# One tile of x turned by the DMA crossbar instead of TensorE, and a gate column read as rows

## The chip, the core and the metric

The kernel runs on one core of a Trainium2 chip. The metric is device time in microseconds of one execution, the median of several runs. The profile is of one further execution; its times count from the start of that execution's span. Five engines have instruction queues of their own: TensorE (PE: matmuls; PEld: its weight loads), VectorE (DVE), ScalarE (ACT), GpSimd (POOL) and SyncE (SP). DMAs are issued from the queues of SP, ACT or POOL and are carried by 16 DMA engines which all queues share.

## The reference

The input x has 2048 tokens of 640 features, in bf16. A linear attention block with 32 heads of 20 features (A) and a gated mixer with an MLP (B) are both computed from x, and a gate per token mixes them.

```python
g = _sigmoid((x * gate_w).sum(-1, keepdims=True))
...
qkv = (x @ wqkv) ...            # (640, 1920)
phi = lambda t: jnp.where(t > 0, t + 1, jnp.exp(t)) + 1e-6
pq, pk = phi(q), phi(k)
kv = jnp.einsum("bhsd,bhse->bhde", pk, v)
z = jnp.einsum("bhsd->bhd", pk)
o = einsum(pq, kv) / (einsum(pq, z)[..., None] + 1e-6)
a = o.reshape(B, S, D) @ wo
...
h = _gelu(_layernorm(x) @ w1)                    # shifted along the tokens in four groups, then @ w2
x1 = x + hs
b = x1 + _gelu(_layernorm(x1) @ w3) @ w4
return g * a + (1 - g) * b
```

For the change it matters that the products x @ wq, x @ wk and the sum x * gate_w all need x with its features on the partitions (turned), because TensorE contracts over partitions.

## The kernel before, in words

The 2048 tokens are cut into 16 x tiles of 128 tokens (x_tok, one tile of 128 tokens by 640 features each). The features are cut into five slices of 128 (KD = 5). The turned form, xT, holds for each slice 128 features on the partitions by all tokens. A Q product of a tile is five pairs of matmuls, one pair per slice: the slice of xT is the stationary operand, and the slice of wq gives 512 and 128 columns (L893 and L894). A K product is the same with wkg, whose last two columns are a column of ones and the gate weights (columns D and D+1), so the K product also gives each token's sum of x and its sum of x * gate_w; ScalarE copies the two to lr for the layer norm and the gate.

The first four x tiles are loaded one by one; tiles 4 to 7, 8 to 11 and 12 to 15 come in three large loads. Tiles 0 to 3 are turned on TensorE: t_x (L758) issues five transposes (L617) into a PSUM bank, and VectorE copies the result to xT (L671). Tiles 4 to 15 are turned by DMA: SP issues a crossbar transpose for each (L703; recorded at L285). The other DMAs are recorded at L289, or at L288 for the gate column.

The order of the first stage is written out by hand. TensorE runs a warm-up of matmuls on constants (L861), transposes tile 0, and then q_four (L900) runs through a list of (tile, slice) entries: an entry (t, None) turns tile t, an entry (t, k) issues the pair of Q matmuls of tile t and slice k, and the stream (L877) calls phi after the fifth slice of a tile. phi is an Exp on ScalarE followed by two operations on VectorE. Then come k_first (L909; recorded at L914) for the K product of tile 0 and k_tile for the others, followed by the Q and K products of tiles 4 to 15. In stream an entry (None, None) issues a small warm-up, which q_four's list does not use.

SP issues in this order: x tiles 0, 1, 2, wq slice 1, x tile 3, wq slices 2 to 4, the five slices of the K weights, the gate column (640 single values, one to each partition and slice), then x tiles 4 to 7 and their transposes, and so on. ScalarE's queue issues wq slice 0 first, and has no other work until the first Exp.

Waits are not written by hand: a small scheduler class records which bytes each operation reads and writes, and puts semaphore waits where they are needed (PSUM banks are locked to the engine that touched them last). Each engine runs its own list in order. A planner (_Items.run) places all later items by modelled times: an item is taken when its inputs are estimated to be ready, so modelled durations of early operations can influence the order of later ones. PSUM banks are also picked by those modelled times.

Of the kernel before, what the change touches and what calls it, by code (L numbers as in the profile page):

```python
# [5 lines left out]
BF16 = mybir.dt.bfloat16  # L6
F32 = mybir.dt.float32
ACTF = mybir.ActivationFunctionType
# [3 lines left out]
D = 640  # L12
# [5 lines left out]
KD = D // 128  # L18
# [398 lines left out]
def _build(nc, A_x, A_wqkv, A_wo, B_w1, B_w2, B_w3, B_w4, gate_w, out, dbg=None, stop=None):  # L417
    sch = _Sched(nc)
# [37 lines left out]
    pa = Arena(SB_LO, SB_HI - SHARED)  # L456
# [3 lines left out]
    ps = nc.alloc_psum_tensor("ps", [128, 8, 512], F32)  # L460
# [6 lines left out]
    ident = pa.alloc("ident", [128, 128], BF16)  # L467
# [11 lines left out]
    x_tok = pa.alloc("x_tok", [128, NT, D], BF16)  # L479
# [10 lines left out]
    junk = pa.alloc("junk", [128, 1, D], BF16)  # L490
    qprod = pa.alloc("qprod", [128, D], F32)
    zacc = qprod
    zsum = pa.alloc("zsum", [128, D], BF16)
    zT = ones_c[:, :].rearrange("p (k f) -> p k f", f=128)
    zf = pa.alloc("zf", [128, KD], BF16)
    xT = ra.alloc("xT", [128, KD, S], BF16)
    GT = ra.alias("GT", [128, KD, D], BF16, ra.last_addr, KD * S * 2)
    wkg = ra.alloc("wkg", [128, KD, NK], BF16)
# [21 lines left out]
    def bank():  # L520
        best = None
        for k_ in range(nbanks[0]):
            b = (bank_rr[0] + k_) % nbanks[0]
            if b in bank_pend or b in bank_hold:
                continue
            lk = sch.locks.get(b)
            tfree = 0.0 if lk is None else sch.ev_time.get((lk[1].sem, lk[1].val), 1e18)
            if best is None or tfree < best[0]:
                best = (tfree, b)
        bank_rr[0] = best[1] + 1  # L530
        bank_pend.add(best[1])
        return best[1]
# [30 lines left out]
    def nfree(ap):  # L563
        n = 1
        for d_ in ap.shape[1:]:
            n *= d_
        return n

    def in_psum(ap):
        return ap.tensor.name == ps.name  # L570

    def act(fn, reads, writes, cost=None):
        if cost is None:
            n = nfree(writes[0])
            cost = max(150.0, 100.0 + 0.833 * n + (70.0 if (reads and in_psum(reads[0])) else 0.0))
            cost += 45.0 * max(0, len(reads) - 1)
        return sch.op("act", fn, reads, writes, cost=cost)
# [13 lines left out]
    def pe(fn, reads, writes, cost=500.0, after=None):  # L591
        for w_ in writes:
            sp_, rl = sch.rects(w_)
            if sp_ == "ps":
                for (_p0, _p1, lo, hi) in rl:
                    for b in range(lo // PS_BANK, (hi - 1) // PS_BANK + 1):
                        bank_pend.discard(b)
        return sch.op("pe", fn, reads, writes, cost=cost, after=after)

    def mm_group(out_ap, pairs, reads_extra=()):  # L600
        n = len(pairs)

        def fn(e, out_ap=out_ap, pairs=pairs, n=n):
            ins = None
            for i, (l, r) in enumerate(pairs):
                ins = e.matmul(out_ap, l, r, start=(i == 0), stop=(i == n - 1))  # L606
            return ins
        reads = [a for p in pairs for a in p] + list(reads_extra)
        return pe(fn, reads, [out_ap], cost=n * (max(nfree(pairs[0][1]), 24) * 0.4167 + 2.5))
# [39 lines left out]
    def activation(out_ap, in_ap, func, scale=1.0, bias=0.0, accum=None):  # L649
        rd = [in_ap] + [a for a in (scale, bias) if not isinstance(a, (int, float))]  # L650
        wr = [out_ap] + ([accum] if accum is not None else [])
        n = nfree(out_ap)
        cost = max(150.0, 100.0 + 0.833 * n + (70.0 if in_psum(in_ap) else 0.0)) + 45.0 * (len(rd) - 1)
        if accum is not None:
            cost += 91.0
        st_ = ACT_SET.get(func)
        if st_ is not None and st_ != sch.act_func:
            cost += 1290.0
            sch.act_func = st_
        if accum is not None:  # L660
            return act(lambda e: e.activation(out_ap, in_ap, func, bias=bias, scale=scale, accum_out=accum), rd, wr, cost=cost)  # L661
        return act(lambda e: e.activation(out_ap, in_ap, func, bias=bias, scale=scale), rd, wr, cost=cost)  # L662

    def memset(engf, ap, val):
        return engf(lambda e: e.memset(ap, val), [], [ap])

    def copy(engf, out_ap, in_ap):
        cost = None
        if engf is dve and in_ap.dtype == BF16 and out_ap.dtype == BF16:
            cost = 65.0 + nfree(out_ap) / 1.92  # L670
        return engf(lambda e: e.tensor_copy(out_ap, in_ap), [in_ap], [out_ap], cost=cost)  # L671
# [7 lines left out]
    def dma_in(out_ap, in_ap, key, **kw):  # L679
        return sch.dma("sp", out_ap, in_ap, key, **kw)  # L680

    def load_x(t, queue="sp"):
        sch.dma(queue, x_tok[:, t, :], x2[128 * t:128 * (t + 1), :], "x%d" % t)

    def load_wq(k, queue="sp"):
        sch.dma(queue, wq[:, k, :], A_wqkv[128 * k:128 * (k + 1), 0:D], "wq%d" % k)

    memset(pool, wkg[:, :, D:D + 2], 1.0)
    load_wq(0, "act")
    for t in range(3):  # L690
        load_x(t)
    load_wq(1)
    load_x(3)
    for k in range(2, KD):
        load_wq(k)
    for k in range(KD):
        dma_in(wkg[:, k, 0:D], A_wqkv[128 * k:128 * (k + 1), D:2 * D], "wk%d" % k)
    dma_in(wkg[:, :, D + 1:D + 2], gate_w.rearrange("(k p o) -> p k o", p=128, o=1), "gw", noncontig=True)
    for c in range(1, NCH):
        for u in {1: (1,), 2: (2, 3)}.get(c, ()):  # L700
            dma_in(x_tok[:, 4 * u:4 * u + 4, :], x2[512 * u:512 * (u + 1), :].rearrange("(n p) d -> p n d", p=128), "xc%d" % u)
        for t in range(4 * c, 4 * c + 4):
            sch.dma("sp", xT[:, :, 128 * t:128 * (t + 1)], x_tok[:, t, :], "trx%d" % (t % 4), transpose=True)  # L703

    k_done = {}

# [49 lines left out]
    WARM2 = 128  # L756
# [94 lines left out]
    def one(n):  # L851
        return nc.const_aps.tensor(1.0, [128, n], BF16)

    def warmup(cols, cyc):
        b = bank()
        steps = [512] * (cols // 512) + [128] * (cols % 512 // 128)

        def fn(e):
            ins = None
            for n in steps:  # L860
                ins = e.matmul(ps[:, b, 0:n], one(128), one(n), start=True, stop=True)  # L861
            return ins
        pe(fn, [], [ps[:, b, :]], cost=cols * cyc)
# [13 lines left out]
    def stream(order, w, n2, done):  # L877
        bs = {}
        for t, k in order:
            if k is None:  # L880
                if t is None:
                    warmup(WARM2, 0.42)
                else:
                    t_x(t)
                continue
            if k == 0:
                bs[t] = pair()
                bank_hold.update((bs[t], bs[t] + 1))
            b = bs[t]
            l = xT[:, k, 128 * t:128 * (t + 1)]  # L890

            def fn(e, l=l, b=b, k=k):
                e.matmul(ps[:, b, 0:512], l, w[:, k, 0:512], start=(k == 0), stop=(k == KD - 1))  # L893
                return e.matmul(ps[:, b + 1, 0:n2], l, w[:, k, 512:512 + n2], start=(k == 0), stop=(k == KD - 1))  # L894
            pe(fn, [w[:, k, 0:512 + n2], l], [ps[:, b, 0:512], ps[:, b + 1, 0:n2]], cost=272.0)
            if k == KD - 1:
                bank_hold.difference_update((b, b + 1))
                done(t, b)

    def q_four():  # L900
        order = [(0, 0), (1, None), (2, None), (1, 0), (0, 1), (1, 1), (2, 0), (2, 1), (3, None), (0, 2), (1, 2), (0, 3), (0, 4), (1, 3),
                 (1, 4), (2, 2), (2, 3), (2, 4), (3, 0), (3, 1), (3, 2), (3, 3), (3, 4)]
        stream(order, wq, 128, lambda t, b: phi(b, pq_tok[:, t + 1, :]))

    def k_out(t, b):
# [16 lines left out]
    addA(("tx", 0), 0.28, lambda: t_x(0, (0, 1, KD)))  # L922
    addA(("warm", 1), 0.0, lambda: warmup(WARM2, 0.42))
    addA(("q", 3), 5.44, q_four)
    addA(("k", 0), 1.36, k_first)
    for i in range(1, 4):
# [349 lines left out]
    for c in range(NCH):  # L1276
        for j in range(KD):
            deps = [(("t1", u), 0.9) for u in range(4 * c, 4 * c + 4)] if j == 0 else []
# [6 lines left out]
    for t in range(NT):  # L1285
        c = t // 4
        deps = [(("w1", c, KD - 1), GEL)]
# [8 lines left out]
    for u in range(NT):  # L1296
        deps = [(("s2", u // 4), 3.2 + 0.9 * (u % 4))]
# [8 lines left out]
    for c in range(NCH):  # L1306
        for j in range(KFF):
            deps = []
# [4 lines left out]
            if j == 0:  # L1313
                deps = deps0 + [(("t2", u), 0.9) for u in range(4 * c, 4 * c + 4)]
# [11 lines left out]
    for t in range(NT):  # L1326
        deps = [(("zb",), 1.0), (("qr", max(t // 4, 1)), 2.0)]
# [14 lines left out]
    for t in range(NT):  # L1342
        c = t // 4
        deps = [(("qt", t), 3.0), (("w4load",), 0.0), (("mq",), 1.0), (("mt",), 2.5)]
# [31 lines left out]
    order = IT.run(sch, hook)  # L1376
# [42 lines left out]
```

## Time and profile before

| | us |
|---|---|
| median of 3 runs | 260.21 |
| lowest, highest | 259.76, 260.26 |
| profiled execution | 260.06 |
| its span | 258.3 |

The time of an execution lies 1.8 us above its span. The granted TensorE clock was 1.0. In the profile's lines, a row of the timeline starts with the start time and the duration in us; "x5" is the number of instructions put together; in brackets stands the idle time before the instruction, and what ended it. A row of waits names the engine, its instruction, what it waited for, and then the total in us, how often, and the longest. A row of DMA issues names destination and source, the queue, how many, the KB of each, and the median us from issue to landing. A row of the table by stretches gives the stretch, the busy time of PE, PEld, DVE, ACT and POOL with their instructions, and last the granted clock, the busy share of the 16 DMA engines (which can pass 1 where packets overlap) and GB/s.

### The profile page before, as it was taken

How to read it: one execution, taken by the hardware profiler on the slowest of the kernel's cores; microseconds unless marked ns; L12 is line 12 of the kernel's file. 1: busy time of each engine (PE TensorE's matmuls, PEld its weight loads, DVE VectorE, ACT ScalarE, POOL GpSimd, SP SyncE). 2: the span in 40 equal slices, each digit the busy share in tenths (PEclk: the TensorE clock that was granted, in tenths of full speed). 3: DMA queues.
4: the chain of work that ended last, by engine and by line, in shares of the span. 5: the costliest groups of instructions: out<-in, count | busy, mean ns of one | idle time of the engine just before them, and what ended most of it. 6: DMA issues, size and time to landing. Idle time of an engine off the chain costs nothing.

```text
span 258.3 us, 3824 instructions
## 1 busy us (share of the span) xinstructions
PE 254.8 (99%) x1427; PEld 122.7 (47%) x1427; DVE 158.2 (61%) x293; ACT 110.9 (43%) x229; POOL 96.8 (37%) x154
## 2 busy tenths in 40 slices
PE   7999999999999999999999999999999999999996
PEld 3555555544444554554444444444444444444443
DVE  2597877899954699989995302999022530134076
ACT  1496777751355857684874240005500045200100
POOL 8014996869934119659681210111020120021000
DMA  6857997826527699483668512114200140000224
GB/s 194 263 101 235 139 141 193 231 55 119 102 49 105 124 392 305 82 101 65 127 124 117 102 20 23 25 25 130 42 3 0 20 124 0 0 0 1 43 84 139
DMA packets 58644, 26.78 MB, mean 104 GB/s; under 512 B 49966, under 2 KB 57215, under 8 KB 58626
## 3 DMA queue, kind: packets, MB, share of 16 engines
q1 hardware_dynamic: 57122, 22.92, 42.5%
q0 software_dynamic: 1168, 3.28, 5.4%
q10 hardware_dynamic: 336, 0.35, 0.4%
q8 instruction: 11, 0.18, 0.3%
q14 instruction: 7, 0.06, 0.1%
HBM read 12.09 MB, written 2.67 MB: 57 GB/s over the span
## 4 chain that ended last, share of the span: by engine, by line
PE 97%; DMA 1%; DVE 0%; issue 0%
PE ps L606 61%; PE ps L1233 22%; PE ps L812 7%; PE ps L893 2%; PE ps L792 1%; DMA x_tok<-in_A_x_dram 1%; PE ps L1120 1%; PE ps L1208 1%; PE ps L617 1%; PE ps L914 1%; PE ps L894 0%; PE ps L984 0%; PE ps L793 0%; PE ps L1213 0%; PE ps L1017 0%; DVE xT L671 0%
## 5 line engine op out<-in xcount | busy, mean ns | idle before, releaser
L606 PE MATMUL ps<-xnT,w 128*128 128x512 bf16 x360 | 81.3, 379 | 0.0
L606 PEld LDWEIGHTS ps<-xnT,w 128*128 128x128 bf16 x360 | 34.6, 98 | 39.3
L645 DVE SCALAR_TENSOR_TENSOR x_tok<-ps,stg,abx 128x512 bf16<-128x512 f32 (+2 forms) x17 | 12.2, 718 | 58.5 <-PE ps L1233 58.4
L1233 PE MATMUL ps<-w,h2T 128*128 128x512 bf16 (+2 forms) x221 | 47.2, 366 | 0.0
L628 POOL TENSOR_SCALAR abx<-x_tok,stg 128x512 f32<-128x512 bf16 x16 | 12.0, 753 | 88.2 <-DVE x_tok L645 70.1
L628 POOL TENSOR_SCALAR xn<-x_tok,st 128x640 bf16<-128x640 bf16 x32 | 38.6, 1215 | 8.6 <-DMA xnT<-xn 8.2
L662 ACT ACTIVATE h2T<-ps 128x512 bf16<-128x512 f32 x52 | 29.9, 599 | 22.7 <-PE ps L606 22.6
L1233 PEld LDWEIGHTS ps<-w,h2T 128*128 128x128 bf16 x221 | 21.2, 98 | 24.1
L662 ACT ACTIVATE tlT<-ps 128x512 bf16<-128x512 f32 x8 | 4.8, 597 | 64.1 <-PE ps L606 41.9
L662 ACT ACTIVATE Er<-ps 128x640 bf16<-128x640 f32 (+1 forms) x35 | 22.9, 658 | 17.8 <-PE ps L606 9.7
L661 ACT ACTIVATE junk<-x_tok 128x640 bf16<-128x640 bf16 x32 | 23.6, 737 | 4.7 <-DVE x_tok L643 4.2
L662 ACT ACTIVATE hsT<-ps 128x512 bf16<-128x512 f32 (+1 forms) x32 | 18.9, 593 | 14.2 <-PE ps L606 13.8
L606 PE MATMUL ps<-w,hsT 128*128 128x512 bf16 (+1 forms) x160 | 24.0, 299 | 0.0
L606 PE MATMUL ps<-wkg,xT 128*128 128x512 bf16 (+1 forms) x150 | 22.6, 299 | 0.0
L606 PE MATMUL ps<-M_sb,pqnT 128*128 128x512 bf16 x80 | 19.7, 379 | 0.0
L606 PEld LDWEIGHTS ps<-w,hsT 128*128 128x128 bf16 x160 | 13.4, 98 | 12.5
L645 DVE SCALAR_TENSOR_TENSOR abx<-ps,stg,abx 128x512 f32<-128x512 f32 x16 | 12.0, 750 | 10.7 <-PE ps L606 7.2
L606 PEld LDWEIGHTS ps<-wkg,xT 128*128 128x128 bf16 x150 | 12.6, 97 | 11.7
L643 DVE SCALAR_TENSOR_TENSOR x_tok<-ps,x_tok 128x640 bf16<-128x640 f32 x16 | 13.1, 821 | 7.6 <-PE ps L606 6.9
L812 PE MATMUL ps<-pk_tok,x_tok 128*128 128x512 bf16 x80 | 17.8, 379 | 0.0
L636 DVE TENSOR_TENSOR qprod<-qprod,pk_tok 128x640 f32<-128x640 f32 x13 | 16.3, 1252 | 0.5
L628 DVE TENSOR_SCALAR Er<-Er 128x640 bf16<-128x640 bf16 (+1 forms) x35 | 11.6, 332 | 7.6 <-ACT Er L662 6.8
(85 smaller groups left out, 282.9 us busy)
## 6 DMA issues: line engine op xcount, KB each, us to landing
w<-in_B_w_dram SPq DMA_DIRECT2D x1, 2160.0 KB, 9.5
w<-in_B_w_dram SPq DMA_DIRECT2D x1, 2080.0 KB, 15.0
x_tok<-in_A_x_dram SPq DMA_DIRECT2D x3, 640.0 KB, 5.6
out_dram<-x_tok SPq DMA_DIRECT2D x3, 640.0 KB, 3.5
w<-in_B_w_dram POOLq DMA_DIRECT2D x8, 160.0 KB, 6.2
wkg<-in_A_wqkv_dram SPq DMA_DIRECT2D x5, 160.0 KB, 3.9
wv<-in_A_wqkv_dram POOLq DMA_DIRECT2D x1, 800.0 KB, 5.6
x_tok<-in_A_x_dram SPq DMA_DIRECT2D x4, 160.0 KB, 3.2
```

Source lines behind the costliest of these rows:

```text
L606: ins = e.matmul(out_ap, l, r, start=(i == 0), stop=(i == n - 1))
L617: ins = e.transpose(o, s_, ident[:])
L628: return engf(lambda e: e.tensor_scalar(out_ap, in_ap, s1, s2, op0, op1), rd, [out_ap], cost=cost)
L636: return engf(lambda e: e.tensor_tensor(out_ap, a, b_, op), [a, b_], [out_ap], cost=cost)
L643: return dve(lambda e: e.scalar_tensor_tensor(out_ap, in0, scalar, in1, op0, op1, accum_out=accum), rd, [out_ap, accum], cost=cost + 70.0)
L645: return dve(lambda e: e.scalar_tensor_tensor(out_ap, in0, scalar, in1, op0, op1), rd, [out_ap], cost=cost)
L661: return act(lambda e: e.activation(out_ap, in_ap, func, bias=bias, scale=scale, accum_out=accum), rd, wr, cost=cost)
L662: return act(lambda e: e.activation(out_ap, in_ap, func, bias=bias, scale=scale), rd, wr, cost=cost)
L792: e.matmul(ps[:, b, :], l, x_tok[:, t, 0:512], start=(t == 0), stop=(t == NT - 1))
L812: ins = e.matmul(ps[:, b, :], l, r, start=(t0 + q_ == 0), stop=(t0 + q_ == NT - 1))
L893: e.matmul(ps[:, b, 0:512], l, w[:, k, 0:512], start=(k == 0), stop=(k == KD - 1))
L1233: ins = e.matmul(o, l, r, start=False, stop=(i == KFF - 1), skip_group_check=shared)
```

## The change

x tile 3 is no longer turned on TensorE. ScalarE's queue issues a crossbar transpose of it, after a small Exp on a constant that brings the load of the activation table to an earlier place. All transposes issued by SP now wait for that one. The Q products of tiles 0 to 2 are reordered and tile 3's come last, as before, in five pairs together.

The gate weights are no longer read into wkg as a column of 640 single values. They are read as five rows of 128 (gw5), from ScalarE's queue behind wq slice 0; one matmul with a 5 by 5 identity turns them into PSUM, and VectorE copies the five columns into wkg. In q_four's list this stands at an entry (None, None), which now means gate_turn.

```diff
+    gw5 = pa.alloc("gw5", [KD, 128], BF16)
...
     load_wq(0, "act")
+    sch.dma("act", gw5[:, :], gate_w.rearrange("(k p) -> k p", p=128), "gw")
     for t in range(3):
         load_x(t)
     load_wq(1)
     load_x(3)
     for k in range(2, KD):
         load_wq(k)
+    activation(junk[:, 0, 0:1], nc.const_aps.tensor(1.0, [128, 1], BF16), ACTF.Exp)
+    turned3 = sch.dma("act", xT[:, :, 384:512], x_tok[:, 3, :], "tr3", transpose=True)
     for k in range(KD):
         dma_in(wkg[:, k, 0:D], A_wqkv[128 * k:128 * (k + 1), D:2 * D], "wk%d" % k)
-    dma_in(wkg[:, :, D + 1:D + 2], gate_w.rearrange("(k p o) -> p k o", p=128, o=1), "gw", noncontig=True)
...
-            sch.dma("sp", xT[:, :, 128 * t:128 * (t + 1)], x_tok[:, t, :], "trx%d" % (t % 4), transpose=True)
+            sch.dma("sp", xT[:, :, 128 * t:128 * (t + 1)], x_tok[:, t, :], "trx%d" % (t % 4), transpose=True, deps=[turned3])
...
                 if t is None:
-                    warmup(WARM2, 0.42)
+                    gate_turn()
...
+    def gate_turn():
+        b = bank()
+        mm_group(ps[:, b, 0:KD], [(gw5[:, :], ident[0:KD, 0:KD])])
+        copy(dve, wkg[:, :, D + 1:D + 2], ps[:, b, 0:KD].unsqueeze(2))
+
     def q_four():
-        order = [(0, 0), (1, None), (2, None), (1, 0), (0, 1), (1, 1), (2, 0), (2, 1), (3, None), (0, 2), (1, 2), (0, 3), (0, 4), (1, 3),
-                 (1, 4), (2, 2), (2, 3), (2, 4), (3, 0), (3, 1), (3, 2), (3, 3), (3, 4)]
+        order = [(0, 0), (1, None), (2, None), (None, None), (1, 0), (0, 1), (1, 1), (2, 0), (2, 1), (0, 2), (1, 2), (2, 2), (0, 3), (1, 3),
+                 (0, 4), (1, 4), (2, 3), (2, 4), (3, 0), (3, 1), (3, 2), (3, 3), (3, 4)]
```

## The prediction

> **What bounds the kernel now.** I read the shares of busy time and the chain that ended last on the page first.
>
> ```profile
> span 258.3 us, 3824 instructions
> PE 254.8 (99%) x1427; PEld 122.7 (47%) x1427; DVE 158.2 (61%) x293; ACT 110.9 (43%) x229; POOL 96.8 (37%) x154
> PE 97%; DMA 1%; DVE 0%; issue 0%
> ```
>
> TensorE is busy for 254.8 of 258.3 us and is 97% of the chain. A microsecond taken off TensorE's stream is worth a microsecond, and so is one of waiting put into it. Next, the waits of TensorE over the whole span:
>
> ```profile
> PE ps L861 <- PEq L1404: 0.8, 1, 0.8
> PE ps L893 <- DVE xT L671: 0.3, 1, 0.3
> PE ps L617 <- DMA x_tok<-in_A_x_dram: 0.2, 1, 0.2
> ```
>
> These are all of them: the start (0.8), x tile 0's arrival (0.2), and one wait for the copy of x tile 1's transposes (0.3, just before 6.21 us). After that TensorE never waits, so nothing downstream can absorb a new wait: it moves the end by its whole length. The change acts in the first 12 us, so I read that part of the timeline.
>
> ```profile
> 5.66 0.89 DVE L671 COPY xT<-ps 128x640 bf16<-128x640 bf16 x2 [0.71 <-PE ps L617]
> 6.21 0.39 PE L893 MATMUL ps<-wq,xT 128*128 128x512 bf16 x1 [0.31 <-DVE xT L671]
> 7.53 0.32 PEld L617 LDWEIGHTS ps<-ident,x_tok 128*128 128x128 bf16 x5
> 7.58 0.44 PE L617 MATMUL ps<-ident,x_tok 128*128 128x128 bf16 x5
> 7.80 0.10 PEld L893 LDWEIGHTS ps<-wq,xT 128*128 128x128 bf16 x1
> 10.25 0.10 PEld L893 LDWEIGHTS ps<-wq,xT 128*128 128x128 bf16 x1
> 10.30 0.38 PE L893 MATMUL ps<-wq,xT 128*128 128x512 bf16 x1
> 11.61 0.37 PEld L914 LDWEIGHTS ps<-wkg,xT 128*128 128x128 bf16 x3
> ```
>
> From 6.21 us on the Q products run in steps of 0.27 us (6.21, 6.49, 6.76 ...), each a 512-column and a 128-column matmul. The five transposes of x tile 3 stand at 7.53 between two steps. Tile 3's own products are the last five of the twenty: their first weight load is at 10.25, and the K products begin at 11.61.
>
> **The change, part by part.**
>
> *Transposes of tile 3 leave TensorE.* Weight loads go on at 7.80 instead of 7.53, and the chain in order of time gives the same piece:
>
> ```profile
> 7.74 0.28 PE ps L617 x5
> ```
>
> I take −0.27 us. The copy after them (0.49 us on VectorE at 8.06) was not waited for, so it is worth nothing. With it gone, tile 3's first weight load would come at 10.25 − 0.27 = 9.98 us.
>
> *The new order of the Q products.* The same twenty pairs are issued, so the sum of work is the same. The third slice of wq is wanted at 7.58 us instead of 7.86, the fourth still at 8.40, the fifth at 8.95 instead of 8.67.
>
> ```profile
> 2.65 0.43 SPq L289 DMA_DIRECT2D x_tok<-in_A_x_dram  x1
> 3.12 1.39 SPq L289 DMA_DIRECT2D wq<-in_A_wqkv_dram  x3
> x_tok<-in_A_x_dram SPq DMA_DIRECT2D x1, 160.0 KB, 4.1
> wq<-in_A_wqkv_dram SPq DMA_DIRECT2D x1, 160.0 KB, 4.1
> ```
>
> Issued at 3.12 and 4.1 us to landing, the third slice is there at 7.2; the later two, about 0.48 us apart, at 7.6 and 8.1. All are 0.3 to 0.8 us early, so the order costs nothing. If that cover went, the loss would be the lateness itself.
>
> *The gate column's matmul.* One weight load and one 5-column matmul come behind tile 2's transposes, which end at about 5.90, inside the 0.31 us in which TensorE waits for the copy. A transpose of 128 columns takes 0.055 us (0.28/5) and a weight load 0.10, so up to 0.15 us fits. Cost: 0. It waits for the gate rows, issued from ScalarE behind wq's first slice, at about 1.24 us. Their landing is bounded by the 2.9 us of x tile 0 and the 4.6 us of the old gate column: 4.1 to 5.9 us. Queued behind that wait is all of TensorE. At the upper end it still costs under 0.1 us. The 5-element copy on VectorE stands behind tile 2's copy (ends 6.55) and ahead of work that starts at 9.88; the nearest copy, 128x128, took 0.22 us. It is hidden, and the K products read its column only after 11 us.
>
> ```profile
> 0.80 0.41 ACTq L289 DMA_DIRECT2D wq<-in_A_wqkv_dram  x1
> 1.24 1.28 ACT L662 ACT_TABLE_LOAD   x1 [1.24 <-PEq L1404]
> 9.15 2.06 ACT L662 ACTIVATE Er<-ps 128x640 bf16<-128x640 f32 x3 [6.62 <-PE ps L894]
> x_tok<-in_A_x_dram SPq DMA_DIRECT2D x1, 160.0 KB, 2.9
> wkg<-in_gate_w_dram SPq DMA_DIRECT2D x1, 1.2 KB, 4.6
> 9.88 0.33 DVE L628 TENSOR_SCALAR Er<-Er 128x640 bf16<-128x640 bf16 x1 [1.33 <-ACT Er L662]
> ```
>
> *ScalarE's queue.* It gets the gate rows' issue (0.41), its table load 0.4 us later, one small Exp, a wait for x tile 3 and the issue of the crossbar transpose (1.3 us on SP). x tile 3 lands at 2.65 + 4.1 = 6.75, so ScalarE is free at about 8.1. Queued behind the wait is the first real Exp, at 9.15 before and about 9.4 now. Hidden, with over a microsecond to spare.
>
> *SP's queue and the 16 DMA engines.* SP loses the gate column's issue, so x tiles 4 to 7 are issued 0.48 us sooner. What the column held back shows in the DMA's rate:
>
> ```profile
> 6.93 0.43 SPq L288 DMA_DIRECT2D wkg<-in_gate_w_dram  x1
> 7.41 0.53 SPq L289 DMA_DIRECT2D x_tok<-in_A_x_dram  x1
> 6.00:9.00 3.00, 2.79 (x24) 1.73 (x25) 1.04 (x3) 0.00 (x0) 1.08 (x1) 1.00 1.06 361
> 9.00:11.00 2.00, 2.00 (x17) 1.12 (x15) 1.08 (x3) 1.79 (x3) 0.00 (x0) 1.00 0.79 182
> 13.22 5.48 SPq L285 DMA_TRANSPOSE xT<-x_tok  x4
> 17.66 1.24 PE L606 MATMUL ps<-wq,xT 128*128 128x512 bf16 x5
> ```
>
> At 182 instead of 361 GB/s (the last column) over 2 us, some 1.0 us of transfer went missing. The new transpose takes about 0.9 us of the same engines (below), so tiles 4 to 7 land about when they did. Their first transpose, issued at 13.22 and landed 2.6 us later, is wanted at 17.66: 1.8 us of slack. The K weights' last slice, issued at about 6.45 with 3.9 us to landing, comes at 10.4, up to 11.3 with the transpose ahead of it, and is wanted after 12 us. SP's later transposes also wait for tile 3's; that ends well before 13 us. All this costs 0.
>
> *When tile 3 arrives.* This term decides, and no row of before has a crossbar transpose beside a full SP queue of plain loads. The nearest rows, alone and beside another queue:
>
> ```profile
> GB/s 126 0 0 0 0 0 0 0 0 112 224 223 215 205 207 73 3 0 0 0 4 140 224 223 215 211 190 56 0 0 0 108 223 223 219 207 203 75 4 0
> q1 hardware_dynamic: 2016, 0.49, 48.1%
> xT<-x_tok SPq DMA_TRANSPOSE x4, 2.7
> xT<-x_tok SPq DMA_TRANSPOSE x1, 2.6
> 25.76 1.29 SPq L285 DMA_TRANSPOSE xT<-x_tok  x1
> w<-in_B_w_dram POOLq DMA_DIRECT2D x1, 160.0 KB, 3.5
> xT<-x_tok SPq DMA_TRANSPOSE x1, 4.3
> 27.10 1.28 SPq L285 DMA_TRANSPOSE xT<-x_tok  x1
> xT<-x_tok SPq DMA_TRANSPOSE x1, 7.2
> ```
>
> The first two lines are the DMA rate over 13.3 to 18.5 us in 40 slices of 0.13 us, and SP's queue in that stretch (2016 packets, 0.49 MB: some 250 bytes each). With nothing beside them, transposes issued from 13.22 on come as bursts of some 0.87 us, the first one 1.25 us after its issue, and land after 2.6 to 2.7 us. With GpSimd's w1 loads on the engines too, the next ones took 4.3 us and 7.2 us.
>
> Here the transpose is issued at about 6.8 us and its burst would begin at about 8.05. SP's queue then still holds most of the K weights and the 640 KB of tiles 4 to 7, 1.3 to 1.4 MB or 4 us at 361 GB/s. So the burst is not alone. **Lower bound** of the landing: 2.6 us, so 9.4 us, and no wait. **Upper bound**: 7.2 us, so 14.0 us, and a wait of 4.0 us. I take 4.3 us, the first transpose beside another queue's loads, as the nearest row (the 7.2 one also stood behind the 4.3 one in its own queue): 6.8 + 4.3 = 11.1 us. It is wanted at 9.98, so TensorE waits 1.1 us, and the K products, in order behind it, wait with it.
>
> A count of packets comes out near: three bursts in 2016 packets are 640 packets and a few each, 40 on each of 16 engines, and a row of a load is 640 bf16 values, 1,280 bytes. If an engine takes one packet from each queue in turn, 40 rows of loads go between them: 40 x 16 x 1,280 B = 0.82 MB, 2.3 us at 361 GB/s, and the landing is 2.6 + 2.3 = 4.9 us. If both queues get equal time, the burst takes 0.87 us more, and the landing is 3.5 us.
>
> [...]
>
> **Sum**, against the profiled execution (260.06 us for a span of 258.3): −0.27 + 1.1 + 0 = +0.83 us, so 260.9 us. That execution is 0.15 us under the median of the runs shown, 260.21. A measurement of this kernel can tell about 0.2%, or 0.52 us, from no change.
>
> **The rivals.**
>
> *Tile 3 is there in time.* Not slower. The transpose goes through the busy engines almost as alone, landing in 2.6 to 3.2 us. For it: lone transposes hardly vary, and each load alone keeps no engine for long. Against it: the rows of 4.3 and 7.2 us, and a DMA share of 1.06 in 6 to 9 us. It decides at a landing of 3.45 us, where the wait is as long as the 0.27 us saved; below 3.2 us the whole saving is kept: 259.8 us.
>
> *Equal time for both queues.* Landing after 3.5 to 3.9 us: a wait of 0.3 to 0.7 us, so 260.1 to 260.5 us, within 0.2%. For it: the plain loads just before and after take 3.9 to 4.1 us in this backlog. Against it: nothing shows the engines sharing by time.
>
> *A long wait.* Landing after 7.2 us as in the second contended row: 260.06 − 0.27 + 4.0 = 263.8 us. For it: the row. Against it: that one stood in line in its own queue, and the loads beside it had smaller pieces.
>
> *The order of later work changes.* The planner places later items by modelled times that move with the new operations. TensorE waits nowhere after 6.21 us, so another order can hardly gain; it could lose some tenths: 260.2 to 261.5 us.
>
> **How the numbers follow.** Forecast (wait of about 0.8 to 1.6 us, 260.6 to 261.4): 0.47. In time: 0.22, of which 0.05 is read as faster, since measured medians scatter by tenths. Equal time: 0.18, 0.16 of it within 0.2%. Long wait: 0.08. Reordering: 0.05, 0.01 of it within 0.2% and 0.01 faster. So faster by over 0.2%: 0.06; within: 0.17 + 0.16 + 0.01 = 0.34; slower: 0.47 + 0.02 + 0.08 + 0.03 = 0.60. The range takes in the in-time case and leaves out the long wait and the scatter below: 259.7 to 261.9 us. The likeliest case alone spans 260.6 to 261.4.
>
> **What the profile after would show.** The five L617 matmuls at 7.58 gone, and the pairs 0.27 us earlier until about 10 us. A TensorE wait of about 1.1 us for a DMA on xT just before the last five L893 pairs; no such row would prove the in-time rival. A transpose on ScalarE's queue at about 6.8 us with 4.3 us to landing. No wait before the small matmul at about 5.9 us and none in the K products; one there would make the sums of the gate rows or of the K weights wrong. A rate near 360 GB/s from 9 us on, less the burst. Any wait of TensorE after 13 us would be the reordering.

## The result, and the profile after

The changed kernel takes 266.92 us (median of 5 runs, 266.51 to 267.06) against 259.97 us before: a ratio of 1.0264, 95% interval 1.025 to 1.0278. It is slower by 6.9 us, where 0.83 us was forecast. The profiled execution shows the same: its span grew from 258.3 to 265.2 us.

From the page of the changed kernel, the span, the busy shares, and the granted clock of TensorE in 40 slices of 6.6 us (9 is full speed):

```profile
span 265.2 us, 3793 instructions
PE 256.4 (97%) x1396; PEld 123.7 (47%) x1423; DVE 158.2 (60%) x293; ACT 111.2 (42%) x230; POOL 96.9 (37%) x154
PEclk9959999999999999999999999999999999999999
```

The page before has no line of clocks; its mean granted clock is 1.0. Here the third slice, 13 to 20 us, is at about half. (27 matmul records are missing from this trace, 1396 against 1423 weight loads; where one is missing the chain of waits strays, so its shares are not used.) The waits of TensorE:

```profile
PE ps L896 <- DMA xT<-x_tok: 3.9, 1, 3.9
PE ps L864 <- PEq L1412: 0.8, 1, 0.8
PE ps L618 <- DMA x_tok<-in_A_x_dram: 0.3, 1, 0.3
PE ps L607 <- DMA xnT<-xn: 0.2, 1, 0.2
PE ps L607 <- ACT h2T L663: 0.2, 1, 0.2
```

The predicted wait is there, at the predicted place, and 3.9 us long instead of 1.1. The two of 0.2 us further down also stand in the trace of a kernel whose time equals that of before (the second run of the gate edit alone), so they explain nothing. The timeline of TensorE around the wait:

```profile
6.27 0.18 PE L607 MATMUL ps<-ident,gw 5*128 5x5 bf16 x1
6.38 0.42 PE L896 MATMUL ps<-wq,xT 128*128 128x512 bf16 x1
10.17 0.22 PE L897 MATMUL ps<-wq,xT 128*128 128x128 bf16 x1
14.31 0.61 PE L896 MATMUL ps<-wq,xT 128*128 128x512 bf16 x1 [3.92 <-DMA xT<-x_tok]
16.95 2.88 PE L922 MATMUL ps<-wkg,xT 128*128 128x512 bf16 x10
```

Five pairs for tile 3 run from 14.31 to 16.95, 2.64 us. Before they took 1.36, from 10.30 to the start of the K products:

```profile
11.66 1.53 PE L914 MATMUL ps<-wkg,xT 128*128 128x512 bf16 x10
```

The chain in order of time shows the same for the K products, first before, then after:

```profile
11.82 1.36 PE ps L914 x10
13.19 4.09 PE ps L606 x30
```

```profile
6.47 7.79 DMA xT<-x_tok
14.31 0.61 PE ps L896
17.16 2.67 PE ps L922 x10
19.83 4.30 PE ps L607 x30
```

Tile 3's first product starts 14.31 − 10.30 = 4.01 us later. Its five pairs lose another 1.28 us, the first K product 1.31, the next stretch 0.21. Together 6.8 of the 6.9 us, all before 24 us. Why the products are slow stands in the table by stretches (the granted clock is the third number from the end):

```profile
12.00:13.00 1.00, 0.00 (x0) 0.00 (x0) 0.97 (x3) 0.00 (x0) 0.00 (x0) 1.00 0.81 213
13.00:14.00 1.00, 0.00 (x0) 0.00 (x0) 0.72 (x1) 0.00 (x0) 0.00 (x0) 0.65 0.35 124
14.00:15.00 1.00, 0.69 (x3) 0.39 (x4) 0.00 (x0) 0.00 (x0) 0.00 (x0) 0.50 0.00 0
19.00:20.00 1.00, 1.00 (x7) 0.69 (x6) 0.11 (x1) 0.13 (x1) 0.00 (x0) 0.50 0.48 94
20.00:21.00 1.00, 1.00 (x6) 0.48 (x5) 0.36 (x2) 1.00 (x3) 0.00 (x0) 0.93 0.72 142
```

The clock falls to 0.5 at about 13.3 us, 2.9 us into the wait, and is back at 20.14 us: 6.84 us at half speed, of which 5.8 us after the wait had ended. Half of that, 2.9 us, is what the products lost.

The other term is the landing of 7.8 us. The packets of ScalarE's queue (q10) and of SP's (q1) in half-microsecond stretches, the first from 8.5 us, the second from 10.0, the third from 11.5:

```profile
DMA packets 152, 0.17 MB, mean 346 GB/s; under 512 B 17, under 2 KB 152, under 8 KB 152
q1 hardware_dynamic: 152, 0.17, 102.2%
...
DMA packets 58, 0.03 MB, mean 58 GB/s; under 512 B 44, under 2 KB 58, under 8 KB 58
q10 hardware_dynamic: 43, 0.01, 39.0%
q1 hardware_dynamic: 15, 0.02, 29.9%
...
DMA packets 173, 0.14 MB, mean 274 GB/s; under 512 B 82, under 2 KB 173, under 8 KB 173
q1 hardware_dynamic: 91, 0.12, 94.5%
q10 hardware_dynamic: 82, 0.02, 20.3%
```

Until 9 us only loads move. Then both queues move together and the sum of them drops: 346, then 58, then 274 GB/s. In the last stretch the two queues pass nearly packet for packet, 91 to 82; over the whole of 9.0 to 12.5 us it is 523 packets of loads to 666 of the transpose. The last six of its 672 packets, 4 bytes each, come only between 13.35 and 13.78 us, four of them in the stretch from 13.5 to 14.0:

```profile
q10 hardware_dynamic: 4, 0.00, 0.5%
```

So the 7.79 us have three parts: 2.54 from the issue to the first packet, 4.77 from the first packet to the last, 0.48 from there to the landing. In the run below in which the transpose is alone they are 1.26, 0.93 and 0.49. It begins late, runs slowly, and ends with a few late packets.

### The profile page after: what moved, and what is told of

Same layout as the page of the kernel before. It is cut to its first block, busy times and chain, and to the rows that moved or that the text cites. A ratio compares the mean times of both kernels' runs of the same rounds, so it can differ in the third digit from the quotient of the medians.

```text
span 265.2 us, 3793 instructions
## 1 busy us (share of the span) xinstructions
PE 256.4 (97%) x1396; PEld 123.7 (47%) x1423; DVE 158.2 (60%) x293; ACT 111.2 (42%) x230; POOL 96.9 (37%) x154
## 4 chain that ended last, share of the span: by engine, by line
PE 78%; DVE 12%; DMA 5%; ACT 2%; SPq 1%; issue 1%; DVEq 0%
PE ps L607 52%; PE ps L1241 21%; DVE qprod L637 7%; DMA xT<-x_tok 3%; DVE x_tok L644 2%; DMA x_tok<-in_A_x_dram 1%; ACT h2T L663 1%; PE ps L922 1%; DMA xnT<-xn 1%; PE ps L795 1%; PE ps L896 1%; PE ps L1128 1%; DVE pq_tok L1155 1%; PE ps L1216 1%; SPq L289 1%
## 5 line engine op out<-in xcount | busy, mean ns | idle before, releaser
L607 PE MATMUL ps<-xnT,w 128*128 128x512 bf16 x350 | 79.9, 379 | 0.7 <-DMA xnT<-xn 0.2
L1241 PE MATMUL ps<-w,h2T 128*128 128x512 bf16 (+2 forms) x215 | 46.4, 366 | 0.3
L607 PE MATMUL ps<-w,hsT 128*128 128x128 bf16 (+1 forms) x159 | 23.8, 298 | 0.1
L607 PE MATMUL ps<-wkg,xT 128*128 128x130 bf16 (+1 forms) x149 | 22.8, 300 | 0.1
L607 PEld LDWEIGHTS ps<-w,hsT 128*128 128x128 bf16 x160 | 13.4, 98 | 12.5
L644 DVE SCALAR_TENSOR_TENSOR x_tok<-ps,x_tok 128x640 bf16<-128x640 f32 x16 | 13.1, 821 | 7.6 <-PE ps L607 7.0
```

What stands on the lines that cost most here:

```text
L644: return dve(lambda e: e.scalar_tensor_tensor(out_ap, in0, scalar, in1, op0, op1, accum_out=accum), rd, [out_ap, accum], cost=cost + 70.0)
L1241: ins = e.matmul(o, l, r, start=False, stop=(i == KFF - 1), skip_group_check=shared)
```

## The experiments

Theory: tile 3's transpose is late because loads of SP's queue stand beside it (A), and its wait costs twice, since the clock falls. Rivals: ScalarE's queue is slow as such (B); a transpose beside loads is slow in whichever queue (C); the clock has another cause. TensorE's later work has the same order in the changed kernel as before, so a changed order was no longer a rival.

**The wait filled.**

```diff
-                 (0, 4), (1, 4), (2, 3), (2, 4), (3, 0), ...
+                 (0, 4), (1, 4), (2, 3), (2, 4), ("fill", None), (3, 0), ...
...
+                elif t == "fill":
+                    warmup(8192, 0.0)
+                    bank_rr[0] = 0
```

> The changed kernel with 16 more matmuls on constants (512 columns, 3.45 us at full clock) ahead of tile 3's Q products, where TensorE waited 3.9 us. They leave the output as it is. Theory (the wait costs twice, once as a wait and once because the granted clock falls to 0.5 for some 6 us after it): tile 3 still lands at about 14.3 us, the clock stays at 1.0, and the time falls by about 2.9 us, to 264.0. Rival (the clock fell for another reason, or its fall costs nothing beside other waits): the clock falls again, or the time stays within 0.5 us of 266.9.

The second added line of the branch sets the pick of PSUM banks back. Measured 264.26 us (263.77 to 264.30), 2.66 us under the changed kernel; ratio to before 1.0155 (1.014 to 1.017). Landing, wait and clock:

```profile
6.89 7.60 DMA xT<-x_tok
```

```profile
PE ps L899 <- DMA xT<-x_tok: 0.8, 1, 0.8
```

```profile
14.00:16.00 2.00, 1.47 (x11) 0.88 (x12) 0.00 (x0) 0.00 (x0) 0.00 (x0) 1.00 0.09 20
```

Tile 3 came no sooner (14.49 us against 14.26), and work that is thrown away made the kernel faster, because the clock stayed at 1.0. The price of the clock is shown.

**Half the fill.** The same edit with warmup(4096, 0.0).

> As the run that filled the wait, with 8 matmuls instead of 16 (1.7 us), so that TensorE is idle for some 2.4 us before tile 3's products instead of 0.8. Theory (the clock falls only where the idle stretch is longer than about 3 us): the clock stays at 1.0 in all runs, 263.8 to 264.6, as with the full fill. Rival (it can fall after about 2 us, depending on when the wait begins, as one run in ten of the transpose from SP's queue hints): the clock falls in some runs, and these take 266 to 267.

Measured 264.46 and 263.34 us at a clock of 1.0, and 265.79 and 265.57 us at a mean clock of 0.994; ratio of the four to before 1.0182 (1.0152 to 1.0213). The profiled run was one of the first two:

```profile
PE ps L899 <- DMA xT<-x_tok: 2.4, 1, 2.4
```

The theory's limit of 3 us (the clock of the changed kernel fell 2.9 us into its wait) is in doubt: with this fill the clock fell in two runs of four. A mean clock of 0.994 over some 263 us is about 3.2 us at half speed, or some 1.6 us lost at most, which fits the two groups if tile 3 landed alike in both. The waits of the two runs in which the clock fell are on no profile; the run of SP's queue, below, shows a fall after a short wait on one.

**The big load afterwards.**

```diff
-            dma_in(x_tok[:, 4 * u:4 * u + 4, :], ..., "xc%d" % u)
+            dma_in(x_tok[:, 4 * u:4 * u + 4, :], ..., "xc%d" % u, deps=[turned3])
```

> The changed kernel with the 640 KB load of x tiles 4 to 7 held until tile 3's transpose has landed; the K weights are still issued ahead. Theory A (packets of another queue's loads go between the transpose's packets, so its length grows with what that queue holds): in place of 7.8 us the landing is about 5 us, since the K weights are through by about 11 us; TensorE's wait is about 1.2 us, the clock stays at 1.0, and the time is 260.5 to 261.5. Theory B (a transpose from ScalarE's queue is slow as such): landing 7 to 8 us, time 266 to 267.

Measured 261.53 us, just past the expected range, ratio 1.0053 (1.0038 to 1.0068).

```profile
6.56 5.30 DMA xT<-x_tok
```

```profile
PE ps L896 <- DMA xT<-x_tok: 1.8, 1, 1.8
```

Without the 640 KB behind the K weights the landing shrinks by 2.5 us, and the clock stays at 1.0 in all runs. Theory A is borne out in kind; the wait was 0.6 us longer than expected. One thing it does not explain. From 10.5 to 11.0 us only two packets of loads move, and the transpose still goes at a fraction of the 214 GB/s that it reaches alone (8.0 to 8.5 us of the run of the transpose alone, below):

```profile
DMA packets 114, 0.03 MB, mean 60 GB/s; under 512 B 113, under 2 KB 114, under 8 KB 114
q10 hardware_dynamic: 112, 0.03, 55.6%
```

So taking turns with the loads is not all of it; what else holds the transpose back is not shown.

**SP's queue.** The same transpose issued by SP, between the K weights and the big load; no wait of the later transposes on it.

```diff
-    turned3 = sch.dma("act", xT[:, :, 384:512], x_tok[:, 3, :], "tr3", transpose=True)
     for k in range(KD):
         dma_in(wkg[:, k, 0:D], ..., "wk%d" % k)
+    turned3 = sch.dma("sp", xT[:, :, 384:512], x_tok[:, 3, :], "tr3", transpose=True)
```

> The changed kernel with tile 3's transpose issued from SP's queue, behind the K weights and ahead of the load of x tiles 4 to 7, so that it is in one queue with the loads. Theory A: in one queue its packets run together behind the K weights (through at about 10.3 us) and ahead of the big load, so it lands at about 11.2 to 11.8 us, 4.4 to 4.9 us after an issue at about 6.95; wait about 1.3 us, time 260.7 to 261.5. Theory C (a transpose beside plain loads is slow in whichever queue): landing 7 to 8 us after the issue, time 266 to 267.5.

Measured 261.10 us, ratio 1.0033 (1.0021 to 1.0046).

```profile
6.95 5.27 DMA xT<-x_tok
```

```profile
12.00:14.00 2.00, 1.73 (x9) 0.88 (x10) 1.62 (x3) 0.00 (x0) 0.00 (x0) 0.77 0.74 250
14.00:16.00 2.00, 2.00 (x7) 0.86 (x6) 0.83 (x2) 0.70 (x1) 0.00 (x0) 0.50 0.40 80
16.00:18.00 2.00, 2.00 (x17) 1.14 (x16) 0.67 (x3) 1.12 (x3) 0.00 (x0) 0.87 0.52 105
```

The landing, 5.3 us, lies between A (4.4 to 4.9) and C (7 to 8), and nearer to A. It is that of the run before this, with the K weights beside it in another queue. So the queue as such does not make it slow; what counts is that the big load now stands behind it. The profiled run took 263.76 us and the nine others 260.5 to 261.6 at a clock of 1.0. In it TensorE waited 1.9 us, and the clock fell at 13.1 us, when the wait was already over, and came back at 16.5. It is the slowest of the ten. The others lie 0.4 to 1.5 us above the 260.06 us of before, which puts their landings at 3.8 to 4.9 us, as an estimate.

**The transpose alone.** The K weights and the big load both wait for it.

> The changed kernel with the K weights and the load of x tiles 4 to 7 both held until tile 3's transpose has landed, so it has the engines nearly to itself from ScalarE's queue. Theories A and C: it lands 2.6 to 3.3 us after its issue, at about 9.1 to 9.8 us, ahead of need, and the new wait is for the K weights, issued from 9.5 us and landing at 12 to 13.5 us where they are wanted from 11.4: some 0.5 to 1.5 us, time 260.3 to 261.5. Theory B: it lands after 7 us all the same, and both waits add up, time above 268.

```profile
6.52 2.68 DMA xT<-x_tok
```

```profile
PE ps L922 <- DMA wkg<-in_A_wqkv_dram: 1.5, 2, 0.8
```

Measured 262.47 us, ratio 1.0089 (1.0074 to 1.0104). From ScalarE's queue it lands after 2.7 us, as the lone ones on SP's queue did before. Theory B is out. The time is worse, and a microsecond above the expected range, because the K weights are late.

**The big load beside it.** The big load is issued ahead, the K weights wait for the transpose.

> The changed kernel with the loads the other way round: x tiles 4 to 7 (640 KB) are issued ahead and stand beside tile 3's transpose, the K weights are held until it has landed. Theory A (it pays for the bytes beside it, whichever they are): with some 600 to 700 KB there, as in the run that held the big load, the landing is 4.5 to 5.5 us. Rival (the big load's four rows per partition are what delays it): 7 us or more. The time is spoilt by the late K weights, 262 to 268, and tells nothing.

```profile
6.52 4.39 DMA xT<-x_tok
```

One run, 263.55 us. The landing is just below what A gave, 4.5 to 5.5. So it is not the form of the big load, four rows to each partition, that delays the transpose. Its first packet moved 2.2 us after the issue.

**The crossbar without the gate edit.** The gate column is read as before, from SP's queue.

> The changed kernel with the gate column read as before, 640 single values from SP's queue between the K weights and the load of x tiles 4 to 7. Theory A (the transpose pays for what the other queue holds beside it): the column adds some 1.0 us of transfer there, so tile 3 lands after 8 to 9.5 us, TensorE waits 4.3 to 5.8 us, the clock falls, and the time is 267 to 269. Rival (the landing is set by the big load alone): 7.5 to 8 us, time within 0.4 us of the changed kernel's 266.9.

The four runs took 266.65, 266.86, 261.89 and 261.81 us; only the two above 266 have a mean clock below 1.0 (0.987 and 0.994). The other two have a ratio of 1.0079 (1.006 to 1.0097) to before. The profiled one is the first.

```profile
6.93 7.79 DMA xT<-x_tok
```

```profile
PE ps L896 <- DMA xT<-x_tok: 4.5, 1, 4.5
```

In the profiled run the landing takes as long as without the column, and the theory's extra microsecond did not come. But the landing is not the same in all four runs. Of the 4.8 us between the first run and the two near 261.9 the clock explains at most 3.4, so tile 3 landed sooner there. These two are 1.8 us above before at a clock of 1.0, which puts their landings at about 5.2 us, as an estimate. The run of 266.86 can owe at most 1.7 us to its clock, so there tile 3 came at least 5.1 us later than before, a landing of some 8.4 us or more, in the theory's range. The same loads stand beside the transpose each time, and why it varies so much is open.

**The gate edit alone**, in the kernel before.

> The kernel before with the gate edit alone: five rows, one matmul, one copy; tile 3 stays on TensorE. Theory: the edit's work is hidden, and the time is within 0.2% of before, 259.7 to 260.6; x tiles 4 to 7 land up to 1 us sooner. Rival (the gate rows ahead of x tile 2 delay the start by the 0.17 us by which the changed kernel's Q products began later): 0.1 to 0.3 us more than before.

Measured 262.05 us, ratio 1.0084 (1.007 to 1.0098): theory and rival were both wrong.

```profile
PE ps L894 <- DVE pq_tok L646: 1.8, 1, 1.8
```

Tile 3's first Q product waited for VectorE to empty the PSUM banks of an earlier tile. One more user of a bank had moved the pick of the later ones. The repeat sets the pick to the banks of the gate's copy and of tile 3's transposes:

```diff
             if k == 0:
+                if t == 3:
+                    bank_rr[0] = 0
                 bs[t] = pair()
```

> The gate edit alone again, now with tile 3's Q products put into the two PSUM banks that the gate's copy and tile 3's copy have left, since in the first run of it TensorE waited 1.8 us for VectorE to empty the banks that were picked. Theory (that wait was the whole loss of 2.2 us): no wait above 0.3 us after 6.3 us, and 259.6 to 260.3. Rival (the gate rows cost something of their own): 260.5 to 262.

Measured 260.14 us against 260.17 before, ratio 1.0000 (0.9992 to 1.0009). That wait was the whole loss, and the gate edit itself costs and brings nothing.

**The K products ahead.** Tile 3's Q products come behind the K products of tiles 0 to 2.

```diff
-    for i in range(1, 4):
+    for i in range(1, 3):
         addA(("k", i), 1.36, lambda t=i: k_tile(t))
+    addA(("q3",), 1.36, lambda: stream([(3, k) for k in range(KD)], wq, 128, ...))
+    addA(("k", 3), 1.36, lambda: k_tile(3))
```

> The changed kernel with the K products of tiles 0 to 2 (4.1 us) put ahead of tile 3's Q products. Tile 3 is then wanted at about 14.4 us instead of 10.4 and lands at 14.3 to 14.5. Theory (the whole loss is the wait and the clock that it costs): the wait is 0 to 0.3 us, perhaps 0.2 us for the last K weights, the clock stays at 1.0, and the time is 259.7 to 260.5. Rival (the transpose also costs something later, through x tiles 4 to 7 landing at 14.5 instead of 13.2): waits for tile 4 or later, 261 or more.

Measured 260.58 us, ratio 1.0030 (1.0019 to 1.0041).

```profile
PE ps L607 <- DMA xT<-x_tok: 0.8, 1, 0.8
PE ps L618 <- DMA x_tok<-in_A_x_dram: 0.6, 2, 0.3
PE ps L922 <- DMA wkg<-in_A_wqkv_dram: 0.2, 1, 0.2
```

The transpose itself still took 7.7 us and is covered now. But the rival has a part too: tile 4's transpose, issued at 14.31 behind the delayed big load, took 4.2 us and landed at 18.49, and the 0.8 us are the wait for it.

**The same with the transpose on SP's queue behind the big load.**

> As the run with the K products ahead, but tile 3's transpose is issued from SP's queue behind the load of x tiles 4 to 7, so that it stands beside no load at all. Theory A: the loads land as in the kernel before or sooner (x tiles 4 to 7 at about 12.3 us), the transpose runs behind them and lands by 13 to 14 us, no wait remains, and the time is 259.6 to 260.0, 0.1 to 0.3 us under the kernel before. Rival (the gain of 0.27 us is eaten by the gate rows or by tile 4's later transpose): 260.0 to 260.5.

Measured 260.28 us, ratio 1.0020 (1.0006 to 1.0035), in the rival's range, but for a reason that neither named. No wait for a transpose remains; the K products, which now start 1.3 us sooner, wait for the last K weights:

```profile
PE ps L923 <- DMA wkg<-in_A_wqkv_dram: 0.6, 1, 0.6
```

**And with x tile 3 loaded behind the K weights.**

> As the run with the K products ahead and the transpose on SP's queue, and x tile 3, which is not wanted before some 13 us now, is loaded behind the K weights instead of among the slices of wq. Theory (0.45 us of transfer less in front of the K weights takes away the 0.6 us for which TensorE waited for them): last K weights by about 10.8 us, no wait, 259.5 to 260.0. Rival (the K weights' landing is late for another reason): a wait of 0.3 to 0.6 us stays, 260.1 to 260.5.

Measured 259.79 us against 260.17 before. The ratio is 0.9996 (0.998 to 1.0011); it lies nearer to 1 than that of the medians, since one of the eleven runs took 261.90. After the start only one wait belongs to the change, and it was there before:

```profile
PE ps L897 <- DVE xT L672: 0.2, 1, 0.2
```

With every new wait gone, the 0.27 us that the change takes off TensorE cannot be told from no change.

## Why the prediction was wrong, point by point

- **What bounds the kernel: right, with one clause wrong.** TensorE's stream sets the time, and nothing downstream absorbed the wait. But "it moves the end by its whole length" failed: a wait of 3.9 us moved the end by 6.8 us, because the clock fell. This is the step that the prediction did not have at all; its 2.7 us (the filled wait) to 2.9 us (the clock's rows) are 40% of the loss. The trace of before, with a clock of 1.0, has no row from which this price could be read. The upper bound of 4.0 us that the prediction gave to the wait had no such price beside it.
- **When tile 3 arrives: the deciding term, mis-sized.** The place, the queue and the direction were right. I took 4.3 us from the nearest row and measured 7.8 us; the row that I kept as the upper bound, 7.2 us, was nearer, and I gave it 0.08. I set it aside because its transpose stood in line in its own queue. The 0.8 to 1.6 us that the forecast gave the wait were my estimate around the 1.1 of the row of 4.3; no run of the changed kernel shows them, and its profile has 3.9. The runs show that the load beside a transpose is what counts: 2.7 us alone, 4.4 with the big load, 5.3 with the K weights, 7.6 to 7.9 with both, each in the profiled runs; other runs of a kernel can differ by a microsecond and more. The burst that was to begin at about 8.05 us, 1.25 after the issue as alone, began at 9.01, 2.54 after it. Why the first packet comes late beside loads is not shown.
- **The count of packets: right in kind, short in rate.** The two queues do pass at something near packet for packet (523 to 666, at best 91 to 82). But I let them move at 361 GB/s together, and from 9.5 to 12.5 us the engines moved 209 GB/s; the late start and the six late packets were in no part of the count. Why the sum drops when transposes and loads mix is not shown by any run.
- **Transposes off TensorE, −0.27 us: right in the rows**, five L617 matmuls gone; as a gain it is below what can be measured, as the last run shows.
- **The order of the Q products and the gate's matmul: nearly free, as predicted.** The first pair after the gate's matmul began at 6.38 instead of 6.21 us: x tile 2 came 0.16 us late, and the gate's matmul ran in front. The small Exp did not bring the load of the activation table forward in time: it began at 1.86 us, against 1.24 before, and no wait of TensorE came of it.
- **The gate edit, 0: right**, by the repeat of the gate edit alone (ratio 1.0000). That it can cost 2 us through the pick of PSUM banks was in no part of the prediction.
- **SP's queue, 0: wrong in its reason.** Tiles 4 to 7 were not to suffer. Their first transpose was issued at 14.57 instead of 13.22, and the late tile 3 hid that; with the wait gone it cost 0.8 us.
- **Later order: nothing.** TensorE's did not change.

## What to carry to other kernels

Price a wait on TensorE by what it does to the clock as well: here 3.9 us of idleness before dense work cost another 2.7 to 2.9 us afterwards. A DMA transpose that lands in 2.7 us alone is to be budgeted with the loads that are in flight beside it, in whichever queue (here 5.3 us beside the K weights, from ScalarE's queue as from SP's, and 7.8 beside the big load as well), and placed behind them or behind enough other products. Where a gain is a quarter of a microsecond, an extra user of a bank or a landing later by a microsecond decides.

## What the runs showed of the hardware

The spells at half clock came in two lengths. By the granted clock they lasted 6.84 us in the changed kernel (13.30 to 20.14), 6.82 us in the profiled run of the crossbar without the gate edit (12.28 to 19.10, its rows below) and 3.41 us in that of SP's queue (13.09 to 16.50): the first two are twice the third.

```profile
12.00:13.00 1.00, 0.00 (x0) 0.00 (x0) 0.97 (x3) 0.00 (x0) 0.00 (x0) 0.64 1.05 260
19.00:20.00 1.00, 1.00 (x9) 0.58 (x8) 0.57 (x1) 0.19 (x1) 0.00 (x0) 0.95 0.69 134
```

In the short spell TensorE was at work again from the start; in the two long ones the wait ran on for 1.0 and 2.5 us into it. The clock fell 2.9 us after TensorE fell idle in the changed kernel, 2.05 us after it in the run without the gate edit, and in the profiled run of SP's queue after a wait of 1.9 us that was already over. Waits of 1.8 and 2.4 us on two other profiles (the big load afterwards, half the fill) left the clock at 1.0. So the length of the wait alone does not separate these runs, and what else decides is not shown.
